# A planner of instruction order: transposing transfers that hold the queue, DRAM stores ordered with their loads, a limit on adding transfers, and new ranks

## The chip, the cores and the metric

The kernel runs on one core of a Trainium2 chip. The metric is the device time of one execution in microseconds (us); the time of a kernel is the median of its runs.

The engines are TensorE (PE in the profile; its weight loads are PEld), VectorE (DVE), ScalarE (ACT), GpSimd (POOL) and SyncE (SP). Each executes its own instructions in the order in which they were written. SP issues nearly all transfers here and POOL the adding ones, so each of them has a queue too.

## The reference

The output is a sum of three terms over x, a matrix of 2048 tokens by 1024 channels:

```python
xn = _layernorm(x, axis=-1)
return x + _A_ref(xn, A_k, A_v, A_shift_k, A_ssm_k, A_ssm_D) + _B_ref(xn, B_w1, B_w2)
```

`_B_ref` is a feed-forward network, silu(xn · w1) · w2 with 3584 inner columns. `_A_ref` has a short causal convolution of k with four taps per channel, a product with v, a long causal convolution over the 2048 tokens per channel (by a Fourier transform of twice the length), and a product with xn:

```python
kv = k_shift * v
...
y_f = kv_f * kf_f[None, :, :, :]
...
y = y + kv * ssm_D[None, None, :]
return q * y
```

All values are 32-bit floats.

## The kernel before

**The work.** The two products of the feed-forward network are done on PE in 16-bit halves: each operand is split into a high and a low part, and each product is three matmuls (high·high, high·low, low·high; lines 1073 to 1075 for the first, 1228 to 1230 for the second). A scheme of seven products instead of eight for blocks of 2 by 2 stands around them, so that sums and differences of rows and of weights are made on DVE, split on ACT (high part) and DVE (low part), partly stored in DRAM (`xspS`, `xspA`, `ws_T`, `ws_B`, `hs`, `w2sP`) and loaded again. The first product's weights come as tiles `raw` (loads from `in_w`); ACT takes their sum of squares (`junk<-raw`), PE sums it over partitions (`ps<-ss,oneb`, line 506), and the split parts are called `wo`. The rows of x are normalised on DVE (`xt`, line 639) and turned on PE (line 658). `ht` and `hf` are tiles of the inner layer and of results.

The long convolution goes over eight groups of 128 channels. For one group `kin` (the padded k) and `kf` (the long filter) are loaded, ACT and DVE apply the taps to get `acc`, v is multiplied in, `hl` holds split parts, some of them turned by a transposing transfer (`hl<-cm`, line 376), PE does a first stage of the transform (lines 1800 to 1802, into `ps`, copied by ACT to `spec` and `tmp`), DVE multiplies the spectra, ACT and DVE split the result (`zh`, `zl`), PE does the inverse (lines 2016 to 2018), and DVE multiplies by the normalised rows `xg` to get `yt`, which POOL adds into `out` in DRAM. A result of the network (`hf`) is added likewise. A stage of the convolution is cut into short pieces that stand between the matmuls of the network; such a stretch, in which spectra are copied, is called a burst below.

**The order.** The program is not written in its final order. Pieces of work are generators ("streams") that yield operations, each an `Op` with its engine, a guess of its time (`busy`), of how much later its result can be read (`late`), what it reads and writes, and its bytes. `Order.run` keeps a clock for every engine, reckons for each stream when its next operation could start, takes the one with the smallest start minus the stream's rank (`bias`), and emits it. So the guesses and the ranks decide the order of every engine's list, and nothing else: what waits for what is decided by semaphores, from the tiles that an instruction reads and writes. The network's matmuls keep their sequence, and other work on PE is put in between.

Helpers make the operations: `L` a load or store on SP (line 355), `X` a transposing transfer on SP (line 376), `G` an adding transfer on POOL (line 380), `V` an operation on DVE (lines 384 and 387), `A` and `a_act` one on ACT (line 397), `T` one on PE. `convolution` starts the streams of the convolution, at the earliest at a time `floor`. In the changed kernel these lines have other numbers: 386, 407, 413, 422, 425 and 435.

Of the kernel before, what the change touches and what calls it, by code (L numbers as in the profile page):

```python
# [20 lines left out]
P = 128  # L21
# [72 lines left out]
class Op:  # L94


    def __init__(self, eng, busy, late, emit, reads, writes, margin, nbytes=0):
        self.eng, self.busy, self.late, self.emit, self.margin = eng, busy, late, emit, margin
        self.reads, self.writes, self.nbytes = reads, writes, nbytes
        self.table = None  # L100
        self.extra, self.rate = 0.0, 0.0


class Stream:
# [5 lines left out]
class Order:  # L110
# [7 lines left out]
    def __init__(self):  # L118
        self.free, self.count = defaultdict(float), defaultdict(int)
        self.wrote, self.read = {}, {}  # L120
        self.slots, self.patterns = {}, {}
        self.streams = []
        self.pipe = self.now = 0.0
        self.table = None

    def cells(self, a):

        if a.space == bass.MemoryType.DRAM:
            return ()
        dims = [tuple(d) for d in a.ap]  # L130
        item = mybir.dt.size(a.dtype)
        key = (a.offset % dims[0][0] if dims[0][0] else 0, tuple(dims[1:]), item)
        if key not in self.patterns:
            offs = np.array([key[0]])
            for step, n in dims[1:]:
                offs = (offs[:, None] + step * np.arange(n)[None, :]).reshape(-1)
# [21 lines left out]

    def prepare(self, s):
        op, t = s.head, -s.head.margin  # L160
        r = [c for a in op.reads for c in self.cells(a)]
# [12 lines left out]

    def run(self):
        while self.streams:
            for s in list(self.streams):
# [141 lines left out]
def h3_ffn_kernel(ctx, tc, x, kp, vs, fs, shift, dskip, w1, w2, cfwd, cinv, out):  # L319
# [26 lines left out]
    def A(f, o, ins, us=None, m=0.15):  # L346
        return Op("ACT", us or 0.1 + size(o) / 1200, 0.2, f, ins, [o], m)

    def T(f, o, ins, us, m=0.2):

        return Op("PE", us, 0.3, f, ins, [o], m)

    def L(o, i, m=0.3):
        n = size(o) * o.shape[0] * mybir.dt.size(o.dtype)
        return later(Op("SP", 0.4, 0.1, lambda: nc.sync.dma_start(o, i), [i], [o], m, n), 0.0, along(o, i, 43.5, 53, 96))

    def later(p, extra, ns):
        p.extra, p.rate = extra, ns * 1e-3 / 16 / 1024
        return p
# [13 lines left out]
    def X(o, i, m=0.3):  # L373

        n = size(o) * o.shape[0] * mybir.dt.size(o.dtype)
        return later(Op("SP", 0.6, 4.0, lambda: nc.sync.dma_start(o, i, transpose=True), [i], [o], m, n), 0.2, 97)

    def G(o, i, m=0.3):
        n = size(i) * i.shape[0] * mybir.dt.size(i.dtype)
        return later(Op("POOL", 1.1, 2.5, lambda: nc.gpsimd.dma_start(o, i, accum_op=ADD), [i], [o], m, n), 0.3,  # L380
                     along(o, i, 83, 119))

    def v_tt(o, a, b, op, **k):
        return V(lambda: nc.vector.tensor_tensor(o, a, b, op=op), o, [a, b], **k)  # L384
# [565 lines left out]
    def quad(i, sp):  # L950
# [26 lines left out]
        add(factors(("S3", "S1"), flat[1], (ltok,)), 0.1)  # L977
        yield v_tt(x, v, x, SUB)
        ltok.set()
        yield v_tt(y, y, x, SUB)  # L980
# [456 lines left out]
    def copies():  # L1437
        n = NT // 2
        for a in range(NT):
            yield flag["unit", a // 2] if a < n else flag["result", a - n + 4]  # L1440
            q = slice(a % n * 2 * P, (a % n + 1) * 2 * P), slice(a // n * W, (a // n + 1) * W)
            o = out[q]
            yield later(Op("SP", 0.4, 0.1, lambda: nc.sync.dma_start(o, x[q]), [], [], 0.3, P * D * 4), 0.0, 43.5)
            flag["copied", a // n].set()

    def squares_w2():
# [92 lines left out]
        flag["all raw"].set()  # L1539

    CLAIM = 5
    SB = 0.04

    def load_w2f():

# [80 lines left out]
                       ap=[list(a.ap[0])] + [list(d) for d in dims] + [[1, n * P]])  # L1626

    TO = (1, 3, 0, 2)
    BETWEEN = (0, 1, 2, 3, 4, 5, None, None, None, 6, 7, None, None, 8, None, None)

    def convolution(floor):
        ra = late.enter_context(tc.tile_pool(name="ra", bufs=1))
# [17 lines left out]
        def rest(floor):  # L1650
# [8 lines left out]
            ctxs["wraw"] = Halves(order, rb, "wraw", 1)  # L1659
            ctxs["squares"] = [(ctxs["wraw"], more["yt"])[:1 + (i < NP // 2)] for i in range(NP)]  # L1660
            add(copies(), 0.3)
            for gen, bias in ((result_parts(), 0.05), (stage1_inv(), 0.03), (norm_rows(), 0.0), (norms_w2(), 0.14)):
                add(gen, bias, max(order.free["DVE"], order.free["ACT"]))

        def loads():
# [376 lines left out]
                if t == tiles2[-1][1]:  # L2042
                    flag["conv out"].set()

        for gen, bias in ((loads(), 0.05), (load_v(), 0.04), (gate(), 0.02), (signal_parts(), 0.07), (parts_of(), 0.14), (stage1(), 0.2),
                          (transforms(), 0.02), (squares_w2(), 0.0), (rest(floor), 0.0)):
# [113 lines left out]
```

## Time and profile before

| what | value |
|---|---|
| median of three runs | 1239.15 us (1236.41 to 1239.62) |
| profiled execution | 1237.35 us, of which the span 1235.6 us |
| busy: PE, DVE, ACT, POOL | 1217.4, 1135.2, 747.2, 143.9 us |
| granted clock of PE | 1.00 |
| transfers | 312.09 MB, 253 GB/s over the span |

The span is the time from the first to the last instruction that the profile shows. Busy time is the sum of an engine's instructions, so an engine can be the bound and still be idle for short waits; those are in the chain of waits and in the brackets of the timeline's rows. Rows of SP marked SPq show when its queue issued a transfer and how long the issue held it, and not when the data landed.

### The profile page before, as it was taken

The page shows a single profiled execution, that of the slowest core. Times are in us where ns is not written, and L with a number is a line of the kernel's source. Part 1 is how long each engine was busy: PE and PEld are TensorE (multiplying, and loading weights), DVE is VectorE, ACT ScalarE, POOL GpSimd, SP SyncE. Part 2 cuts the span into 40 slices and gives each one's busy share as a digit, 9 for nine tenths or more (in the row PEclk, how much of TensorE's full clock was granted, in tenths as well). Part 3 has the DMA queues.
Part 4 walks back from the last instruction along what each step waited for, and adds up shares of the span by engine and source line. Part 5 has one row for each costly group of instructions (what it writes and reads, how often), then busy time and mean ns, then how long its engine had stood idle before and what let it go on. Part 6 is the DMA issues. An engine that isn't in the chain of part 4 may idle for free.

```text
span 1235.6 us, 17325 instructions
## 1 busy us (share of the span) xinstructions
PE 1217.4 (99%) x6092; PEld 591.3 (48%) x6093; DVE 1135.2 (92%) x1414; ACT 747.2 (60%) x1299; POOL 143.9 (12%) x164
## 2 busy tenths in 40 slices
PE   8999998999999999999999999999999999999998
PEld 7644444444444454445444444454444445445445
DVE  7998995988799989999999999999998997997993
ACT  7867886887767796767764464353345337336232
POOL 2000000000000020001110130021013014112213
PEclk9999999999999999999999999999999999999999
DMA  9368889889999999987999899989969978776667
GB/s 339 108 208 308 295 299 306 279 267 317 337 371 307 286 252 305 271 238 223 306 361 282 262 296 286 236 222 285 279 142 234 331 164 198 179 159 131 152 144 140
DMA packets 264295, 312.09 MB, mean 253 GB/s; under 512 B 49424, under 2 KB 175632, under 8 KB 261136
## 3 DMA queue, kind: packets, MB, share of 16 engines
q1 hardware_dynamic: 237616, 286.33, 73.0%
q0 software_dynamic: 26592, 24.65, 14.4%
q8 instruction: 47, 0.77, 0.2%
q14 instruction: 40, 0.33, 0.1%
HBM read 198.20 MB, written 112.72 MB: 252 GB/s over the span
## 4 chain that ended last, share of the span: by engine, by line
PE 59%; DVE 19%; DMA 10%; issue 6%; ACT 5%; POOL 1%; SPq 0%; ACTq 0%; DVEq 0%; POOLq 0%
PE ff L1075 9%; PE ff L1073 9%; PE ff L1074 9%; PE ff L1228 9%; PE ff L1229 9%; PE ff L1230 9%; DVE spec L384 5%; DVE wo L387 2%; DMA raw<-in_w 2%; DMA hsfA<-ht 2%; DVE ht L387 2%; DVE tmp L384 1%; PE ps L1800 1%; PE ps L1802 1%; PE ps L1801 1%
## 5 line engine op out<-in xcount | busy, mean ns | idle before, releaser
L1075 PE MATMUL ff<-x,wo 128*128 128x512 f16 (+2 forms) x840 | 306.8, 367 | 2.3 <-DVE wo L387 2.3
L1074 PE MATMUL ff<-x,wo 128*128 128x512 f16 (+2 forms) x840 | 306.8, 367 | 1.4 <-DVE x L387 1.4
L1073 PE MATMUL ff<-x,wo 128*128 128x512 f16 (+2 forms) x840 | 306.7, 367 | 0.7 <-ACT wo L397 0.4
L1228 PE MATMUL ff<-x,wo 128*128 128x512 f16 x778 | 292.3, 376 | 0.4 <-ACT hf L397 0.4
L1229 PE MATMUL ff<-x,wo 128*128 128x512 f16 x778 | 292.3, 376 | 0.0
L1230 PE MATMUL ff<-x,wo 128*128 128x512 f16 x778 | 292.2, 376 | 0.0
L384 DVE TENSOR_TENSOR spec<-spec 128x512 f32<-128x512 f32 (+1 forms) x280 | 246.1, 914 | 0.7
L1230 PEld LDWEIGHTS <-wo 128*128 128x128 f16 x860 | 84.1, 98 | 99.4
L1228 PEld LDWEIGHTS <-wo 128*128 128x128 f16 x860 | 84.1, 98 | 98.9 <-issue 0.2
L1229 PEld LDWEIGHTS <-wo 128*128 128x128 f16 x860 | 84.1, 98 | 98.1 <-issue 0.6
L1075 PEld LDWEIGHTS <-wo 128*128 128x128 f16 x840 | 82.1, 98 | 95.0 <-DVE wo L387 3.1
L1073 PEld LDWEIGHTS <-wo 128*128 128x128 f16 x840 | 82.1, 98 | 92.1 <-issue 3.4
L1074 PEld LDWEIGHTS <-wo 128*128 128x128 f16 x840 | 82.1, 98 | 87.1 <-issue 1.2
L380 POOL DMA_DIRECT2D out<-yt x62 | 68.9, 1323 | 346.9 <-DVE yt L387 322.9
L380 POOL DMA_DIRECT2D out<-hf x61 | 56.7, 929 | 421.5 <-ACT hf L397 324.2
L397 ACT ACTIVATE hf<-ff,invc 128x512 f32<-128x512 f32 x62 | 42.2, 681 | 94.9 <-PE ff L1230 76.3
L384 DVE TENSOR_TENSOR tmp<-spec 128x2048 f32<-128x2048 f32 (+1 forms) x48 | 92.2, 1931 | 0.5
L384 DVE TENSOR_TENSOR spec<-tmp 128x512 f32<-128x512 f32 (+1 forms) x96 | 80.1, 864 | 0.5
L387 DVE SCALAR_TENSOR_TENSOR ht<-hf,wsc,ht 128x1024 f16<-128x1024 f32 (+1 forms) x56 | 65.3, 1166 | 10.7 <-ACT ht L397 8.0
L387 DVE SCALAR_TENSOR_TENSOR wo<-raw,wsc,wo 128x512 f16<-128x512 f32 (+1 forms) x56 | 56.2, 1013 | 14.2 <-ACT wo L397 13.9
L397 ACT ACTIVATE ht<-hf,wsc 128x1024 f16<-128x1024 f32 (+1 forms) x56 | 59.0, 1054 | 8.8 <-DVE hf L384 4.3
L397 ACT ACTIVATE spec<-spec 128x1024 bf16<-128x1024 f32 x32 | 33.7, 1054 | 50.1 <-DVE spec L384 41.0
(193 smaller groups left out, 1869.4 us busy)
## 6 DMA issues: line engine op xcount, KB each, us to landing
wo<-hs SPq DMA_DIRECT2D x128, 256.0 KB, 5.3
wraw<-in_w SPq DMA_DIRECT2D x33, 512.0 KB, 6.1
hs<-ht SPq DMA_DIRECT2D x64, 256.0 KB, 4.8
out<-hf POOLq DMA_DIRECT2D x61, 256.0 KB, 5.2
raw<-in_w SPq DMA_DIRECT2D x28, 512.0 KB, 6.1
kin<-in_kp SPq DMA_DIRECT2D x16, 704.0 KB, 6.4
w2sP<-wo SPq DMA_DIRECT2D x42, 256.0 KB, 4.4
kf<-in_fs SPq DMA_DIRECT2D x8, 1024.0 KB, 6.4
```

Of the source, the lines that this page charges most:

```text
L380: return later(Op("POOL", 1.1, 2.5, lambda: nc.gpsimd.dma_start(o, i, accum_op=ADD), [i], [o], m, n), 0.3, along(o, i, 83, 119))
L384: return V(lambda: nc.vector.tensor_tensor(o, a, b, op=op), o, [a, b], **k)
L387: p = V(lambda: nc.vector.scalar_tensor_tensor(o, a, s, b, op0=op0, op1=op1), o, [a, b] + ([] if isinstance(s, float) else [s]), **k)
L397: nc.scalar.activation(o, i, func, scale=scale, **kw)
L1073: nc.tensor.matmul(o, w[:, 0, k], xf[:, :, k, 0], start=first and k == 0, stop=False, **kw)
L1074: nc.tensor.matmul(o, w[:, 0, k], xf[:, :, k, 1], start=False, stop=False, **kw)
L1075: nc.tensor.matmul(o, w[:, 1, k], xf[:, :, k, 0], start=False, stop=last and k == KH - 1, **kw)
L1228: nc.tensor.matmul(o, hx[:, 0, :], wc[:, 0, q], start=begin, stop=False, **kw)
L1229: nc.tensor.matmul(o, hx[:, 0, :], wc[:, 1, q], start=False, stop=False, **kw)
L1230: nc.tensor.matmul(o, hx[:, 1, :], wc[:, 0, q], start=False, stop=end, **kw)
L1800: nc.tensor.matmul(o, cf[:, 0], hi[i], start=i == 0, stop=False, **kw)
L1801: nc.tensor.matmul(o, cf[:, 0], lo[i], start=False, stop=False, **kw)
```

## The change

The change touches the planner alone: its guesses, its ranks, and what it takes for a dependence. The instructions are the same ones, save three fewer of the spare matmuls with which PE is kept busy at the start; their order differs. There are four parts.

- DRAM: the planner's list of what was read and written (`cells`) knew on-chip memory only. Now stores to scratch tensors and to `out` count too, with `dram`, so that a load of what was stored is planned behind its store. An adding transfer is planned behind the copy of x into `out` (`after`).
- Adding transfers: at most 768 rows of them are planned in flight (`room`, `ring`).
- Guesses: a transposing transfer has 1.3 instead of 0.6 us on SP, and holds SP in the plan until the transfers ahead of it have drained (`held`); loads 0.5 instead of 0.4; adding transfers 0.6 instead of 1.1 on POOL.
- Ranks: many `bias` values, and the table `BETWEEN`, which sets between which matmuls the pieces of the first transform stage stand. `convolution` now starts only when the last reads of the pools that it replaces are planned to be over.

```diff
     def cells(self, a):
 
+        dims = [tuple(d) for d in a.ap]
         if a.space == bass.MemoryType.DRAM:
-            return ()
-        dims = [tuple(d) for d in a.ap]
+            return self.dram(a, dims)
...
+    def dram(self, a, dims):
+
+        name = a.tensor.name
+        if name.startswith("in_"):
+            return ()
+        if name.startswith("out_"):
+            row, col = divmod(a.offset, D)
+            if dims[0][0] == D:
+                return [("copied", row // (2 * P), col // W)]
+            at = [(row % T2 + T2 // 2 * i, row // HALF) for i in range(2 if len(dims) > 2 else 1)]
+            return [(name, t, b, col // P + c) for t, b in at for c in range(max(1, dims[-1][1] // P))]
+        offs = {a.offset + P * i for i in range((dims[-1][1] + P - 1) // P)}
+        for step, k in dims[:-1]:
+            if k != P:
+                offs = {o + step * i for o in offs for i in range(k)}
+        return [(name, o) for o in offs]
...
+    def room(self, t, rows):
+
+        held = [q for q in self.ring if q[0] > t]
+        while held and sum(n for _, n in held) + rows > 6 * P:
+            t = max(t, held.pop(0)[0] + 0.3)
+        return t
...
                     t = max(self.free[e] + late, s.at)
+                    if s.head.rows:
+                        t = self.room(t, s.head.rows)
...
+                if op.held:
+                    op.busy = max(op.busy, self.pipe - 0.35 - t)
+                if op.rows:
+                    self.ring = [q for q in self.ring if q[0] > t] + [(end, op.rows)]
...
-    def T(f, o, ins, us, m=0.2):
+    def T(f, o, ins, us, m=0.1):
...
-        return later(Op("SP", 0.4, 0.1, lambda: nc.sync.dma_start(o, i), [i], [o], m, n), 0.0, along(o, i, 43.5, 53, 96))
+        return later(Op("SP", 0.5, 0.1, lambda: nc.sync.dma_start(o, i), [i], [o], m, n), 0.0, along(o, i, 43.5, 53, 96))
...
-        return later(Op("SP", 0.6, 4.0, lambda: nc.sync.dma_start(o, i, transpose=True), [i], [o], m, n), 0.2, 97)
+        p = later(Op("SP", 1.3, 3.3, lambda: nc.sync.dma_start(o, i, transpose=True), [i], [o], m, n), 0.2, 97)
+        p.held = True
+        return p
...
-            yield (0.25, 0.2, 0.1, 0.14)[min(n, 3)]
+            yield (0.25, 0.2, 0.1, 0.04)[min(n, 3)]
...
-    BETWEEN = (0, 1, 2, 3, 4, 5, None, None, None, 6, 7, None, None, 8, None, None)
+    BETWEEN = (0, 1, 2, None, 3, 4, 5, None, 6, None, 7, None, None, 8, None, None)
...
-            for gen, bias in ((result_parts(), 0.05), (stage1_inv(), 0.03), (norm_rows(), 0.0), (norms_w2(), 0.14)):
+            for gen, bias in ((result_parts(), 0.05), (stage1_inv(), 0.03), (norm_rows(), 0.05), (norms_w2(), 0.3)):
...
-        convolution(max(order.free["DVE"], order.free["ACT"]))
+        ids = {id(r) for r in (xts_r, sums_r, s1_r, xst_r)}
+        left = [t for k, t in order.read.items() if isinstance(k[0], tuple) and k[0][0] in ids]
+        convolution(max([order.free["DVE"], order.free["ACT"]] + left))
...
-        add(more_rows(), 0.0)
+        add(more_rows(), 0.3)
...
-    add(transposes(), 0.05)
+    add(transposes(), 0.0)
...
-    add(factors_w1(), 0.1)
-    add(spill_w1(), 0.04)
+    add(factors_w1(), 0.05)
+    add(spill_w1(), 0.02)
```

What this does to the lists is shown at three places. In their rows a name with a number is a tile, `A<-B` is written from read, and x2 stands for two alike in succession.

The first is SP's list at the start of the convolution, near 190 us of the profile before. Before:

```order
L355 DMA ws_T_125<-wo_205 128x1024
L355 DMA raw_2157<-in_w 128x4x256
L355 DMA xspA_155<-xst_2079 128x1024
L355 DMA xspS_157<-xst_2080 128x1024
L355 DMA kin<-in_kp 128x1408
L355 DMA hs_88<-ht_214 128x4x256 x2
L355 DMA kf<-in_fs 128x2048
L355 DMA raw_2210<-in_w 128x4x256
L355 DMA ws_T_126<-wo_209 128x1024
L355 DMA ws_B_127<-wo_205 128x1024
L355 DMA hs_89<-ht_215 128x4x256 x2
```

After:

```order
L386 DMA raw_2152<-in_w 128x4x256
L386 DMA xspS_153<-xst_2050 128x1024
L386 DMA xspA_155<-xst_2081 128x1024
L386 DMA xspS_157<-xst_2082 128x1024
L386 DMA hs_88<-ht_214 128x4x256 x2
L386 DMA raw_2205<-in_w 128x4x256
L386 DMA ws_T_126<-wo_206 128x1024
L386 DMA ws_B_127<-wo_207 128x1024
L386 DMA kin<-in_kp 128x1408
L386 DMA hs_89<-ht_215 128x4x256 x2
L386 DMA kf<-in_fs 128x2048
```

The second `raw` of these rows stood behind kin, a pair of hs stores and kf, and now stands ahead of kin and kf, right behind the pair; one spill store (`xspS_153`) moved behind the first `raw`.

The second is ACT's list in the fifth burst of the convolution (group 4, near 930 us). Before:

```order
L397 ACTIVATE tmp<-ps_8187 128x2x256
L397 ACTIVATE tmp<-ps_8192 128x2x256
L397 ACTIVATE xg_8152<-xg_8152,nmr,rstd 128x128
L397 ACTIVATE spec<-ps_8187 128x2x256
L397 ACTIVATE xg_8152<-xg_8152,nmr,rstd 128x128
L397 ACTIVATE spec<-ps_8192 128x2x256
L397 ACTIVATE tmp<-ff_8224 128x2x256
L397 ACTIVATE xg_8152<-xg_8152,nmr,rstd 128x128 x2
L397 ACTIVATE tmp<-ps_8231 128x2x256
L397 ACTIVATE spec<-ff_8224 128x2x256
```

After:

```order
L435 ACTIVATE tmp<-ps_8204 128x2x256
L435 ACTIVATE tmp<-ps_8209 128x2x256
L435 ACTIVATE spec<-ps_8204 128x2x256
L435 ACTIVATE spec<-ps_8209 128x2x256
L435 ACTIVATE tmp<-ff_8239 128x2x256
L435 ACTIVATE tmp<-ps_8245 128x2x256
L435 ACTIVATE spec<-ff_8239 128x2x256
L435 ACTIVATE spec<-ps_8245 128x2x256
L435 ACTIVATE xg_8257<-xg_8257,nmr,rstd 128x128 x2
```

The rows of xg, which wait for a load, stood among the copies of the transform's results, and now stand behind all of them. In the burst of group 3 it is the other way round: there all four xg rows stood ahead of the last two copies only, and now two of them stand ahead of eight copies, and two ahead of the last four; the load of these two stands on SP behind a transposing transfer and the load of kf.

The third is DVE's list at the start, near 10 us. Before:

```order
L602 BN_STATS st<-xt_249 128x6
L387 SCALAR_TENSOR_TENSOR x_232<-ft_309,x_232 128x4x128
L602 BN_STATS st<-xt_249 128x6
L545 TENSOR_SCALAR pow_322<-ft_321 128x1
L547 RECIPROCAL pow_322<-pow_322 128x1
L605 BN_AGGR ln_226<-st 128x2
L387 SCALAR_TENSOR_TENSOR x_233<-ft_329,x_233 128x4x128
L639 TENSOR_SCALAR xt_249<-xt_249,ln_226 128x1024
L387 SCALAR_TENSOR_TENSOR wo_205<-x_238,wsc,wo_205 128x512
L602 BN_STATS st<-xt_263 128x6 x2
L387 SCALAR_TENSOR_TENSOR wo_205<-x_238,wsc,wo_205 128x512
```

After:

```order
L640 BN_STATS st<-xt_251 128x6 x2
L583 TENSOR_SCALAR pow_315<-ft_314 128x1
L585 RECIPROCAL pow_315<-pow_315 128x1
L643 BN_AGGR ln_226<-st 128x2
L425 SCALAR_TENSOR_TENSOR x_232<-ft_298,x_232 128x4x128
L425 SCALAR_TENSOR_TENSOR x_233<-ft_322,x_233 128x4x128
L677 TENSOR_SCALAR xt_251<-xt_251,ln_226 128x1024
L425 SCALAR_TENSOR_TENSOR wo_205<-x_238,wsc,wo_205 128x512 x2
```

The second half of the row's statistics (BN_STATS) moved ahead of the split of x, and those of the next row are no longer between the two wo rows.

At the tail, SP's list ended in two xg loads, two loads `hf<-out` and two xg loads, and now has the second pair of xg between the two `hf<-out`. On DVE and ACT near 70 us, the split of ht stood ahead of a split wo, and now stands behind it. In the list of PE the pieces of the convolution and the turns of rows stand at other places between the network's matmuls, by up to some microseconds of matmul work.

More of the change, by code (lines that the diff above doesn't have):

```diff
@@ L100, in __init__ @@
         self.table = None
-        self.extra, self.rate = 0.0, 0.0
+        self.extra, self.rate, self.rows, self.held, self.after = 0.0, 0.0, 0, False, []
 class Stream:
@@ L123, in __init__ @@
         self.pipe = self.now = 0.0
+        self.ring = []
         self.table = None
     def cells(self, a):
+        dims = [tuple(d) for d in a.ap]
         if a.space == bass.MemoryType.DRAM:
-            return ()
-        dims = [tuple(d) for d in a.ap]
+            return self.dram(a, dims)
         item = mybir.dt.size(a.dtype)
@@ L160, in prepare @@
         op, t = s.head, -s.head.margin
-        r = [c for a in op.reads for c in self.cells(a)]
+        r = [c for a in op.reads for c in self.cells(a)] + op.after
         w = [c for a in op.writes for c in self.cells(a)]
@@ L375, in X @@
         n = size(o) * o.shape[0] * mybir.dt.size(o.dtype)
-        return later(Op("SP", 0.6, 4.0, lambda: nc.sync.dma_start(o, i, transpose=True), [i], [o], m, n), 0.2, 97)
+        p = later(Op("SP", 1.3, 3.3, lambda: nc.sync.dma_start(o, i, transpose=True), [i], [o], m, n), 0.2, 97)
+        p.held = True
+        return p
     def G(o, i, m=0.3):
         n = size(i) * i.shape[0] * mybir.dt.size(i.dtype)
-        return later(Op("POOL", 1.1, 2.5, lambda: nc.gpsimd.dma_start(o, i, accum_op=ADD), [i], [o], m, n), 0.3,
-                     along(o, i, 83, 119))
+        p = later(Op("POOL", 0.6, 3.0, lambda: nc.gpsimd.dma_start(o, i, accum_op=ADD), [i], [o], m, n), 0.3,
+                  along(o, i, 83, 119))
+        p.rows = n // (mybir.dt.size(o.dtype) * o.shape[-1])
+        if o.space == bass.MemoryType.DRAM:
+            row, col = divmod(o.offset, D)
+            p.after = [("copied", row // HALF * (NT // 4) + a, col // W) for a in range(NT // 4)]
+        return p
     def v_tt(o, a, b, op, **k):
@@ L976, in quad @@
         yield v_tt(z, x, z, SUB)
-        add(factors(("S3", "S1"), flat[1], (ltok,)), 0.1)
+        add(factors(("S3", "S1"), flat[1], (ltok,)), 0.07)
         yield v_tt(x, v, x, SUB)
@@ L1442, in copies @@
             o = out[q]
-            yield later(Op("SP", 0.4, 0.1, lambda: nc.sync.dma_start(o, x[q]), [], [], 0.3, P * D * 4), 0.0, 43.5)
+            yield later(Op("SP", 0.6, 0.1, lambda: nc.sync.dma_start(o, x[q]), [], [o], 0.3, P * D * 4), 0.0, 43.5)
             flag["copied", a // n].set()
@@ L1541, in h3_ffn_kernel @@
     CLAIM = 5
-    SB = 0.04
+    SB = 0.07
     def load_w2f():
@@ L2043, in gated @@
                     flag["conv out"].set()
-        for gen, bias in ((loads(), 0.05), (load_v(), 0.04), (gate(), 0.02), (signal_parts(), 0.07), (parts_of(), 0.14), (stage1(), 0.2),
+        for gen, bias in ((loads(), 0.05), (load_v(), 0.04), (gate(), 0.02), (signal_parts(), 0.07), (parts_of(), 0.1), (stage1(), 0.2),
                           (transforms(), 0.02), (squares_w2(), 0.0), (rest(floor), 0.0)):
```

## Prediction

> **What bounds the kernel now.** I read the page first: its busy times, then the waits of TensorE (PE), then the stretches, and then the rows at each wait.
>
> ```profile
> span 1235.6 us, 17325 instructions
> ...
> PE 1217.4 (99%) x6092; PEld 591.3 (48%) x6093; DVE 1135.2 (92%) x1414; ACT 747.2 (60%) x1299; POOL 143.9 (12%) x164
> ```
>
> PE is the bound, with 18.2 us of the span in which it isn't busy. An order can win only there, at a clock that is full in every stretch that I show. The waits of PE (line, what it waited for, total us, times, longest) name where most of these 18 us lie:
>
> ```profile
> PE ps L506 <- ACT junk L397: 3.1, 1, 3.1
> PE ff L1075 <- DVE wo L387: 2.3, 3, 1.3
> PE ps L1800 <- DVE tmp L384: 1.6, 1, 1.6
> PE ff L1074 <- DVE x L387: 1.4, 2, 1.0
> PE ft L658 <- DVE xt L639: 1.0, 2, 0.8
> PE ps L2017 <- DVE zl L387: 0.8, 1, 0.8
> PE ps L1800 <- ACT spec L397: 0.8, 1, 0.8
> PE ft L658 <- DVE s L387: 0.7, 2, 0.4
> PE ft L658 <- ACT xt L397: 0.7, 1, 0.7
> PE ff L1228 <- ACT hf L397: 0.4, 1, 0.4
> ```
>
> These ten are 12.8 us, and none is a transfer: each is VectorE (DVE) or ScalarE (ACT) being late, sometimes because a transfer held them. The second limit is DVE, by stretches (us, then busy time and count of PE, PEld, DVE, ACT, POOL, the granted clock, the DMA share, GB/s):
>
> ```profile
> 210.00:330.00 120.00, 120.00 (x562) 54.40 (x560) 103.45 (x139) 98.45 (x164) 0.76 (x1) 1.00 0.95 297
> 330.00:480.00 150.00, 149.75 (x719) 70.09 (x718) 143.28 (x161) 114.98 (x197) 9.70 (x9) 1.00 1.01 310
> 480.00:780.00 300.00, 299.23 (x1440) 140.18 (x1438) 294.29 (x342) 181.77 (x309) 33.21 (x34) 1.00 0.95 278
> ```
>
> From 210 to 480 us PE is full and DVE has 23 us free; from 480 to 780 us DVE has 5.7 us left in 300.
>
> **The change part by part.** It adds and removes no work but three spare warm-up matmuls on a PE that waits there anyhow (cost zero, and covered by the wait for the first data). Every other instruction stays; the planner's guesses and ranks only put it elsewhere. So the sum goes by waits that open or close.
>
> *The load behind kin (208 us).* First the rows of SyncE (SP, start and us), whose queue issues the loads, then ACT's (in brackets its idle time before and what ended it), PE's, and the page's row on this kind of load (KB each, median us to landing):
>
> ```profile
> 189.19 0.43 SPq L355 DMA_DIRECT2D xspS<-xst  x1
> 194.75 0.33 SPq L355 DMA_DIRECT2D kin<-in_kp  x1
> 195.17 0.93 SPq L355 DMA_DIRECT2D hs<-ht  x2
> 196.16 0.66 SPq L355 DMA_DIRECT2D kf<-in_fs  x1
> 196.91 1.05 SPq L355 DMA_DIRECT2D raw<-in_w  x1
> ```
>
> ```profile
> 206.94 1.06 ACT L397 ACTIVATE junk<-raw 128x1024 bf16<-128x1024 f32 x1 [7.09 <-DMA raw<-in_w]
> ```
>
> ```profile
> 204.66 0.38 PE L1075 MATMUL ff<-x,wo 128*128 128x512 f16 x1
> 208.14 0.16 PE L506 MATMUL ps<-ss,oneb 128*128 128x2 bf16 x1 [3.10 <-ACT junk L397]
> ```
>
> ```profile
> raw<-in_w SPq DMA_DIRECT2D x28, 512.0 KB, 6.1
> ```
>
> SP stands from 189.62 to 194.75 before kin, because kin takes memory of the last spill store; raw goes out four places behind it, lands after 10.0 us (196.91 to 206.94) where the median of its 28 kind is 6.1, and ACT stands idle 7.09. In the new order raw goes ahead of kin, right behind the first hs pair. Its issue then is near 191.5, an estimate: 189.19 + 0.43, plus the hs pair of 0.93, plus the wait for its producer. It lands at 197.6 (median) to 201.5 (the 10.0 us of this row); junk ends 1.06 later, by 202.6 at the latest, and PE comes there at 204.88 (204.66 and one step of the 0.216 at which these matmuls start). The wait is gone: 3.1 by the row. Ends: 0 (if another producer is as late) and 3.1. I take **−3.1**. kin and kf then go out last. The first to read either is ACT's square of kf:
>
> ```profile
> 212.01 1.06 ACT L397 ACTIVATE hl<-kf 128x1024 bf16<-128x1024 f32 x1 [0.89 <-issue]
> ```
>
> It stands 15.9 us behind kf's issue, and kf moves by three rows of under 1 us each, so I cost that at nothing.
>
> *The start.* DVE:
>
> ```profile
> 10.34 0.69 DVE L387 SCALAR_TENSOR_TENSOR x<-ft,x 128x512 f16<-128x512 f32 x1 [0.56 <-ACT xt L397]
> 14.76 1.28 DVE L602 BATCH_NORM_STATS2 st<-xt 128x6 f32<-128x512 f32 x2
> 15.95 0.73 DVE L387 SCALAR_TENSOR_TENSOR wo<-x,wsc,wo 128x512 f16<-128x512 f32 x1
> ```
>
> The second half of a row's statistics now fills the 0.56, and the 1.28 of the next row's stand behind the wo split that PE waits for (L1075 and L1074: 3.7 in five waits, two of the wo ones and one x before 21 us). DVE gains up to 1.84 at 15.95, but ACT's part of the split and the loads come no earlier. Ends 0 and −1.8; the middle, **−0.9**.
>
> *Row ht ahead of wo (70 us).*
>
> ```profile
> 68.86 1.28 DVE L387 SCALAR_TENSOR_TENSOR ht<-hf,wsc,ht 128x1024 f16<-128x1024 f32 x1
> 70.04 1.29 DVE L387 SCALAR_TENSOR_TENSOR wo<-raw,wsc,wo 128x1024 f16<-128x1024 f32 x1
> ```
>
> PE waits 1.3 for this wo (longest of L1075). It now stands ahead of ht on DVE and ACT, worth 1.18 (70.04 − 68.86) if its input is there. Ends 0 and −1.3; **−0.8**, nearer the row. What is late next is ht, whose readers are transfers.
>
> *Transposes (L658).* They wait 2.4 us in five places; the new order puts most of them 2 to 5 us of matmul time later, while new places arise. Ends +0.7 (the longest again) and −2.4; I take **−0.5**.
>
> *Bursts of the convolution* (stage 1, products and inverse of one channel group follow on one another). Group 4, ACT and then PE:
>
> ```profile
> 932.12 0.49 ACT L397 ACTIVATE xg<-xg,nmr,rstd 128x128 f32<-128x128 f32 x1 [3.13 <-DMA xg<-in_x]
> 933.87 0.38 PE L1800 MATMUL ps<-hl,cfw 128*128 128x512 f16 x1 [1.61 <-DVE tmp L384]
> ```
>
> ACT waits in order for a gate row xg while copies of PE's results (spec, tmp) stand behind it, and PE waits for those. In the new order all copies of that burst stand ahead of the xg rows: **−1.6** (ends 0 and −1.6). For the 0.8 at zl, PE comes 2.6 to 3.2 us of matmul time later to the same DVE work: **−0.7**. For the 0.8 at spec the place on PE is the same and DVE has slightly less ahead of it: **−0.4**, ends +0.8 and −0.8.
>
> *The tail.*
>
> ```profile
> 1210.40 7.31 SPq L355 DMA_DIRECT2D hf<-out  x2
> 1217.82 1.20 SPq L355 DMA_DIRECT2D xg<-in_x  x2
> 1222.68 0.88 ACT L397 ACTIVATE xg<-xg,nmr,rstd 128x128 f32<-128x128 f32 x2 [0.23 <-DMA xg<-in_x]
> 1223.46 0.67 ACT L397 ACTIVATE hf<-ff,invc 128x512 f32<-128x512 f32 x1
> ```
>
> The second hf load waits for an addition into out to land; the second xg pair stands behind it, and ACT's hf copy, for which PE waits 0.4, behind that. The pair now goes out between the two hf loads: **−0.4** (ends 0 and −0.4).
>
> *New waits.* No row shows them. The nearest row for an order of this kind is this one's own list: of its 12.8 us, 8.4 go above, and 4.4 stay. I let a fifth of what goes come back elsewhere, **+1.7**; ends 0 and all of it, +8.4.
>
> The limit on rows of adding transfers and the order of DRAM stores act on the list only; POOL's 143.9 us busy of 1235.6 can hide a later addition. Raising a transposing transfer's time on SP moves it and its neighbours by a place or so, costed at nothing at the x loads behind, and at its worst in the rivals.
>
> Sum: −3.1 −0.9 −0.8 −0.5 −1.6 −0.7 −0.4 −0.4 +1.7 = −6.7. The profiled run took 1237.35 for a span of 1235.6; with the change 1230.65. The median of the runs is 1239.15, 1.8 above the profiled one, so the forecast is **1232.4**.
>
> **The rivals.** A (gives back): PE comes 5.3 us earlier (the terms before 330 us) to a stretch in which DVE has 5.7 us free in 300. If DVE is what sets the pace there, the lead ends at a burst, as a longer wait for spec, zl or tmp: −6.7 + 5.3 = −1.4, so 1237.8. For it speaks the 294.29 of 300; against it the 23 us that DVE has free from 210 to 480, in which the earlier start can be taken along.
>
> B (slower): a transposing transfer holds SP, and a load that ACT needs inside a burst stands behind it.
>
> ```profile
> 310.37 9.67 SPq L376 DMA_TRANSPOSE hl<-cm  x1
> 704.51 1.52 SPq L376 DMA_TRANSPOSE hl<-cm  x1
> 716.51 0.88 ACT L397 ACTIVATE xg<-xg,nmr,rstd 128x128 f32<-128x128 f32 x2 [0.34 <-DMA xg<-in_x]
> ```
>
> These are two holds on SP and, of group 3 before, ACT's xg row. In group 3 the new order puts the second xg load behind a transposing one and the 1 MB kf, and its row on ACT ahead of the burst's last four copies; before, the xg rows stood ahead of the last two alone. With the usual 1.5 nothing is lost; with 9.67 SP and ACT are 8.15 later, and of an ACT wait of 3.13 PE saw 1.61 at 933 us, so 1.5 is hidden and 6.6 reaches PE. Slower by more than 3.7 needs 10.4 on top of the sum, so two such holds (13.2): −6.7 + 13.2 = +6.5, 1245.7; one gives 1239. Against it: at 704 us, in this very group, the hold was 1.52. [...]
>
> C (another producer is as late at 208 us): the first term falls, −3.6, 1235.5. Against it the ACT row, idle 7.09 for raw alone.
>
> D (nothing happens): the terms are moved by less than they are worth, 1239. The five terms above that rest on a named place in the order are against it.
>
> **How the numbers follow.** About 0.3%, 3.7 us, is what a measurement of this kernel can tell from no change. Forecast, −10 to −4 us: 0.60, and 0.06 more beyond it; A 0.17; C 0.05; D 0.04; B 0.08. Faster: forecast with what lies beyond (0.66) and half of C, 0.68; slower: B, 0.08, and some of the +8.4 end of new waits, 0.10 in all; the rest, 0.22, is within. The range from 1226.9 (every term at its gaining end and no new wait, −12.2) to 1239.5 (D, or one hold of B) leaves 2 in 10 out.
>
> **What would show it.** In the profile after: ACT's 7.09 and PE's 3.1 at 208 us are gone, with raw ahead of kin on SP; no xg row of ACT idles inside group 4's burst; the first matmul waits before 21 us are shorter by near 1; hf at the tail doesn't wait for xg; DVE's busy time stays at 1135. It is wrong if PE's waits for spec, tmp, zl or wo between 480 and 1000 us grow by more than 3 us (A or B), or if SP's transposing rows of 5 us and more stand ahead of an xg that ACT waits for.

## The result and the profile after

The changed kernel took 1232.66 us (median of six runs, 1229.4 to 1233.87), the kernel before beside it 1239.18 (1236.41 to 1241.98): a ratio of 0.9945, 95% interval 0.9927 to 0.9963. That is 6.5 us less; 1232.4 had been forecast. The profiled execution of the changed kernel took 1233.5 for a span of 1231.7, so the two profiles are only 3.9 us apart. The page of the changed kernel (span; busy time, share and count by engine), and then PE's waits:

```profile
span 1231.7 us, 17303 instructions
...
PE 1215.8 (99%) x6089; PEld 590.7 (48%) x6090; DVE 1136.5 (92%) x1414; ACT 750.8 (61%) x1299; POOL 143.7 (12%) x164
```

```profile
PE ff L1111 <- ACT hf L435: 2.6, 4, 1.2
PE ff L1112 <- DVE x L425: 2.2, 3, 0.9
PE ft L696 <- DVE xt L677: 2.0, 1, 2.0
PE ff L1113 <- DVE wo L425: 1.5, 3, 0.8
PE ps L1838 <- DVE yt L425: 1.3, 1, 1.3
```

The waits for junk (3.1 us), tmp (1.6), zl and spec (0.8 each) are gone from the list. The waits for hf (2.6), yt (1.3) and xt (2.0, at 9.45 us, ahead of the network's first matmul) are new or longer. At 208 us SP's rows show raw ahead of kin and kf, and ACT has no idle time for it (its row stands below them):

```profile
190.72 1.59 SPq L386 DMA_DIRECT2D hs<-ht  x2
192.40 0.74 SPq L386 DMA_DIRECT2D raw<-in_w  x1
193.19 0.84 SPq L386 DMA_DIRECT2D ws_T<-wo  x1
194.12 0.46 SPq L386 DMA_DIRECT2D ws_B<-wo  x1
195.75 0.33 SPq L386 DMA_DIRECT2D kin<-in_kp  x1
```

```profile
198.62 1.06 ACT L435 ACTIVATE junk<-raw 128x1024 bf16<-128x1024 f32 x1
```

One pair of profiles doesn't show where the time went, because single executions of one order differ by up to 2.7 us in a stretch. The experiments below leave most of either order as it was, and so each gave one more execution of it. The table has the time between the same two matmuls of the network, taken from the timelines (in the first row, from the start of the span to such a matmul); a stretch is named by its place in the profile before. A star marks a stretch that the edit of that run changes, left out of the last column.

| stretch, us | before | before_less_dve, xg_last (order of before) | after | raw_last, after_less_dve (order of after) | means, after − before |
|---|---|---|---|---|---|
| 0 to 29 | 28.34 | 28.38, 28.23 | 28.14 | 26.82, 26.92 | −1.0 |
| 29 to 54 | 25.72 | 25.71, 25.71 | 26.87 | 26.86, 26.86 | +1.15 |
| 54 to 87 | 32.04 | 32.04, 32.04 | 30.98 | 30.98, 30.98 | −1.06 |
| 87 to 195 | 108.64 | 107.08, 109.59 | 109.01 | 107.91, 107.32 | −0.4 |
| 195 to 238 | 43.24 | 45.03, 42.63 | 39.98 | 48.75*, 39.98 | −3.65 |
| 238 to 485 | 246.19 | 248.01*, 248.88 | 246.72 | 247.23, 246.59* | −0.6 |
| 485 to 510 | 25.10 | 25.06*, 25.11 | 26.85 | 27.07, 25.06* | +1.86 |
| 510 to 691 | 181.60 | 181.60, 181.61 | 181.69 | 181.56, 181.56 | 0.0 |
| 691 to 741 | 50.20 | 50.61, 50.79 | 51.04 | 50.34, 53.01* | +0.2 |
| 741 to 914 | 172.20 | 172.61, 171.74 | 171.74 | 171.74, 171.74 | −0.4 |
| 914 to 949 | 35.06 | 34.44, 32.62* | 32.22 | 32.22, 32.22 | −2.5 |
| 949 to the end | 280.43 | 281.11, 282.58 | 279.91 | 280.89, 279.91 | −1.1 |

The last column adds up to about −7.5 us, where the medians are 6.5 apart; with two or three executions of each order, whose stretches differ by up to 2.7 us, it can't be closer. Most of it comes from two places, near 208 and near 933 us, and 1 us each from the start and from 70 us; 1.15 us is lost at 30 us and 1.9 at 490 us.

### The profile page after: what moved, and what is told of

The parts are those of the page before. It is cut to its first block, busy times and chain, and to the rows that moved or that the text cites. A ratio compares the mean times of both kernels' runs of the same rounds, so it can differ in the third digit from the quotient of the medians.

```text
span 1231.7 us, 17303 instructions
## 1 busy us (share of the span) xinstructions
PE 1215.8 (99%) x6089; PEld 590.7 (48%) x6090; DVE 1136.5 (92%) x1414; ACT 750.8 (61%) x1299; POOL 143.7 (12%) x164
## 4 chain that ended last, share of the span: by engine, by line
PE 71%; DVE 11%; issue 8%; DMA 6%; ACT 3%; POOL 1%; SPq 0%; DVEq 0%; POOLq 0%; ACTq 0%
PE ff L1266 12%; PE ff L1268 12%; PE ff L1267 12%; PE ff L1111 9%; PE ff L1113 9%; PE ff L1112 9%; PE ps L1838 2%; PE ps L1840 2%; PE ps L1839 2%; DMA raw<-in_w 2%; DVE spec L422 2%; DVE x L425 1%; DVE ht L425 1%; DVE wo L425 1%; DMA out<-yt 1%
## 5 line engine op out<-in xcount | busy, mean ns | idle before, releaser
L413 POOL DMA_DIRECT2D out<-hf x61 | 54.2, 888 | 420.4 <-ACT hf L435 323.5
L425 DVE SCALAR_TENSOR_TENSOR acc<-kin,taps,acc 128x1024 f32<-128x1024 f32 x48 | 61.3, 1277 | 1.4 <-ACT acc L435 1.3
```

The lines of the kernel that those rows point to most:

```text
L413: p = later(Op("POOL", 0.6, 3.0, lambda: nc.gpsimd.dma_start(o, i, accum_op=ADD), [i], [o], m, n), 0.3, along(o, i, 83, 119))
L425: p = V(lambda: nc.vector.scalar_tensor_tensor(o, a, s, b, op0=op0, op1=op1), o, [a, b] + ([] if isinstance(s, float) else [s]), **k)
```

## The experiments

Those that move one instruction use a small addition to the planner: the plan is made as ever, and a marked operation is emitted only when so many later operations of an engine have gone out. All other rows keep their places. Line numbers in these kernels are larger by the lines added.

```diff
-            op.emit()
+            self.send(op)      # emits op, or keeps it until p.hold = (engine, n) is counted down
```

### The load behind kin

**raw_first**, one move in the kernel before:

```diff
-                    yield L(kin, kp[g, b])
+                    yield hold(L(kin, kp[g, b]), "SP", 3) if (g, b) == (0, 0) else L(kin, kp[g, b])
...
-                        yield L(kf, fs[g])
+                        yield hold(L(kf, fs[g]), "SP", 1) if g == 0 else L(kf, fs[g])
```

> The kernel before with one move: on SP, kin and kf of the first group stand behind the raw load that PE waits for at 208 us; every other row of every engine is in its place. Theory 'terms add' (a wait taken away before 330 us stays away): PE's wait of 3.1 us at ps (sum of squares) is gone, ACT's 7.09 too, and the kernel is 3 us faster (1236). Rival 'given back': PE comes 3 us earlier to 460 to 505 us, DVE does not, and PE waits there for ACT's hf or DVE; the kernel is 0 to 1 us faster. Rival 'another producer' (C of the prediction): the wait stays, on another name, no change.

Measured: 0.9995 of before (0.9982 to 1.0009), so no change. The wait at 208 is gone. Nine us later PE stands for 2.53 us. ACT's and PE's rows of raw_first:

```profile
211.61 1.06 ACT L415 ACTIVATE hl<-kf 128x1024 bf16<-128x1024 f32 x1 [5.00 <-issue]
```

```profile
216.97 0.38 PE L1091 MATMUL ff<-x,wo 128*128 128x512 f16 x1 [2.53 <-ACT hf L415]
```

ACT now reaches its square of kf early and stands there until 211.61. The profile names nothing that it waits for. What lies just ahead is POOL's addition of a row into kf, issued at 205.72, after kf had landed. Of this addition the second row below gives the time from issue to landing, 5.8 us, so it lands at 211.5, and the square starts at 211.61:

```profile
205.72 1.03 POOL L394 DMA_DIRECT2D kf<-in_dskip  x1 [104.91 <-DMA hs<-ht]
...
kf<-in_dskip POOLq DMA_DIRECT2D x1, 0.5 KB, 5.8
```

In the kernel before it is the same: the addition is issued at 206.15 and takes 5.8 us, and the square starts at 212.01.

All later rows of ACT, the copy hf among them, stand behind that square. Of the three expectations the second and third had the time right, but the lead was lost at 217 us and not at 460.

**raw_and_square** moves that square ten rows later on ACT as well:

```diff
+                    yield hold(p, "ACT", 10) if (g, a) == (0, 0) else p
```

> The kernel before with two moves: raw ahead of kin and kf on SP (as in raw_first), and on ACT the first square of kf ten rows later, where the changed kernel has it. In raw_first PE's wait at 208 us was gone and one of 2.69 us at 216.97 stood in its place, for hf, behind that square, which waited for POOL's addition into kf until 211.6. Theory 'the kf chain held ACT': the wait near 217 us goes to under 0.5, and 3 us of the lead hold at least to 330 us. Whether they hold to the end: 'terms add' 1237 against 1240 before, a ratio of 0.9975; 'given back at 460 to 505' a ratio of 0.9995 with 2 to 3 us of waits for hf there. If ACT is late for another reason, a wait of 2 us or more is left at 217.

Measured: 1.0001 (0.9986 to 1.0016). PE again waits, 2.51 us at 216.05, because the next raw load is now the late one, as ACT's row shows:

```profile
213.76 1.06 ACT L415 ACTIVATE junk<-raw 128x1024 bf16<-128x1024 f32 x1 [4.61 <-DMA raw<-in_w]
```

In this profile, the slowest of its twelve executions (1243.34 against a median of 1239.3), PE also ran at half its clock behind the wait (0.50 from 217.10 to 220.51, which is 1.7 us more; the last section has the rows).

**kin_late** holds kin and kf back until that pair of raw loads is out too (12 and 10 issues instead of 3 and 1).

> The kernel before with kin and kf of the first group held on SP until three raw loads have gone out (twelve and ten issues later), and the first square of kf ten rows later on ACT; nothing else moves. In raw_and_square the second pair of raw loads was the next to be late (213.76, behind 1.7 MB of kin and kf). Theory 'the loads share one supply, and the last of the row is late': both waits (208 and 216 us) are under 0.5, the lead near 230 us is 5 us (2.7 more than raw_and_square and 3.2 more than before). Rival: the square of kf, now waiting for its late load and POOL's addition, holds ACT and a wait of 2 to 4 us stands near 220. By the end, 2 to 3 us faster (0.998) if the lead is kept, 1.000 if it is given back between 330 and 505 us.

Measured: 0.9990 (0.9974 to 1.0006). The stretch from 195 to 238 us took 41.43 us, against 43.24 before, 44.33 in raw_and_square and 39.98 after. A wait of 1.29 us was left at 221.13. So the stretch is 1.8 us shorter than before, where I had expected 3.2: three moves together bring half of what the changed order has here. In this run POOL's addition also goes out only behind the two squares of kf (218.8 against 217.4 and 218.4), so that they don't wait for it. By the time alone the run can't be told from the kernel before.

**raw_last** undoes the move in the changed kernel: its raw load is held back for six issues, behind kin and kf.

```diff
+            yield hold(p, "SP", 6) if (n, a) == (10, 1) else p
```

> The changed kernel with the same move undone: its raw load stands behind kin and kf again, nothing else moves. 'Terms add': 3 us slower than the changed kernel, about 1236. 'Given back': PE's wait at 208 us is back with 3 us, the waits for hf between 460 and 505 us (2.9 us) are gone, and the time stays that of the changed kernel, 1232 to 1233.

Measured: 1.0012 of before (0.9997 to 1.0028), where the changed kernel is at 0.9945. The loss is over twice what either theory gave: 8.8 us in the stretch. The waits for hf between 460 and 505 us are not gone, as 'given back' has it, but as long as in the changed kernel (27.07 in that stretch). PE's row, and then its clock by stretches (us, busy time of the engines, the granted clock, the DMA share, GB/s):

```profile
205.14 0.16 PE L562 MATMUL ps<-ss,oneb 128*128 128x2 bf16 x1 [5.49 <-ACT junk L453]
```

```profile
205.00:211.00 6.00, 5.54 (x14) 1.97 (x14) 4.56 (x9) 3.10 (x10) 0.00 (x0) 0.50 0.49 138
211.00:214.00 3.00, 3.00 (x15) 1.37 (x14) 1.59 (x2) 2.26 (x3) 0.00 (x0) 0.99 0.77 221
```

The wait itself is 5.5 us, and after it PE runs for 6 us at half its clock, which is 3 us more. So in the changed order this one position is worth 8.8 us, and in the order of before it is worth nothing that the time shows: there the wait only goes on to the next late row.

**left_only** and **no_left**: the later start of the convolution alone in the kernel before, and the changed kernel without it. Both are planned anew.

```diff
-        convolution(max(order.free["DVE"], order.free["ACT"]))
+        convolution(max([order.free["DVE"], order.free["ACT"]] + left))
```

> The kernel before with one part of the change alone: the streams of the convolution start only when the last reads of the pools that they replace are planned to be over; ranks, guesses and DRAM order are those of before. It moves raw ahead of kin and starts the convolution's ACT rows later, and the whole order behind is planned anew. If this part carries the gain at 208 us, PE's wait there is gone and none stands at 217; by itself 3 to 5 us faster than before (ratio 0.996 to 0.9975) where nothing new opens, and 0.9990 to 1.000 where it is given back.

> The changed kernel without the later start of the convolution alone (its raw load stands behind kin and kf again, as in before), all else as changed, planned anew. If that part carries most of the gain: PE's wait at 208 us is back with 3 us or more, with some us at half clock if it is longer than 3.4, and the ratio to before is 0.998 to 1.000. If ranks and guesses carry it: 0.995 to 0.997 as the changed kernel.

Measured: 1.0077 (1.0056 to 1.0098) and 1.0072 (1.0045 to 1.0099): both are 9 us slower than before. Both expectations missed. In no_left raw does stand behind kin and kf, but PE's wait there is only 0.32 us (at 204.39). The 3.4 us of its expectation lie between two measured pauses, 3.26 in the kernel before (full clock behind it) and 3.43 in before_less_dve (half clock); a wait of 0.32 says nothing on it. In left_only the gain at 208 us is there (3.3 us by 213 us of before); half of it is gone by 230, nearly all by 400, and by 640 us the run is 12 us behind, in waits for hf, tmp and x. The later start is not a part that carries the gain by itself; as both runs have another order throughout, they don't show what it is worth inside the changed one.

### Where time is lost near 490 us

**after_less_dve** and **before_less_dve** leave out four of the six additions of taps of group 2 (5.1 us of DVE near 470 to 490 us), in the changed kernel and in the one before:

```diff
+                        if g == 2 and j > 0:
+                            p.emit = lambda: None
```

> The changed kernel without four of the six additions of taps of group 2 on DVE (between 467 and 490 us, 1.28 us each, 5.1 us of DVE; they are left out of the result). If DVE sets the pace from 460 to 505 us, PE's waits for hf there (2.9 us) shrink to under 0.7 and the kernel is 2 to 3 us faster than the changed one (about 1230). If ACT's own row of copies makes them, they stay within 0.5 us and so does the time.

> The kernel before without the same four additions of taps of group 2. PE has no wait of over 0.2 us between 460 and 700 us there, so if DVE is late only when PE leads, nothing changes (1239, within 1 us). If less DVE work helps in any case (later bursts come earlier), it is 1 to 2 us faster.

Measured: 0.9918 (0.9899 to 0.9937) and 0.9998 (0.9983 to 1.0013). In the changed kernel the waits for hf go, all but one of 0.85 us, and the stretch from 485 to 510 is back at 25.06. In the order of before nothing comes of it. So DVE sets the pace there in the changed order and not in the order of before. That it does so because PE leads, which is rival A's mechanism, is another matter: in raw_last PE comes to this place 6.9 us later than in the changed kernel and 4.4 us later than in the kernel before (the matmul at 485.03 of before, at 489.41), and its waits for hf are all there. So it is the order, and not the lead. By time the run is about 3 us below the changed kernel, with intervals that overlap; by the profile part of the lead is given back at the burst near 712 us, where PE now waits 2.6 us for yt instead of 1.3.

```profile
PE ps L1841 <- DVE yt L425: 2.6, 1, 2.6
PE ff L1112 <- DVE x L425: 2.2, 3, 0.9
PE ff L1113 <- DVE wo L425: 2.0, 4, 0.8
...
PE ff L1111 <- DVE hf L422: 0.8, 1, 0.8
```

The rows for x and wo are waits ahead of 71 us. The wait for yt has a cause of its own in the changed kernel, by DVE's rows at both places:

```profile
462.81 0.75 DVE L425 SCALAR_TENSOR_TENSOR yt<-ps,csc,xg 128x512 f32<-128x512 f32 x1 [2.85 <-DMA xg<-in_x]
...
714.77 0.75 DVE L425 SCALAR_TENSOR_TENSOR yt<-ps,csc,xg 128x512 f32<-128x512 f32 x1 [2.24 <-DMA out<-yt]
```

The second names the addition of the previous yt into out. There is one buffer for yt, in two halves, and DVE can't write it before POOL's transfer has read it. For the first the profile names an xg load, but its tile had been normalised by 457.4, and what ends just ahead of the row is again an addition: issued at 454.25, it landed at 462.63. (The second was issued at 705.89 and landed at 714.68.) The same row in raw_last, and in the kernel before:

```profile
469.67 0.75 DVE L439 SCALAR_TENSOR_TENSOR yt<-ps,csc,xg 128x512 f32<-128x512 f32 x1 [3.35 <-DMA xg<-in_x]
...
458.87 0.75 DVE L387 SCALAR_TENSOR_TENSOR yt<-ps,csc,xg 128x512 f32<-128x512 f32 x1 [0.39 <-DMA out<-yt]
```

In the six executions of the order of before this addition took 4.7 to 6.4 us from issue to landing, and DVE stood 0.29 to 2.05 us; in three of the changed order it took 8.4 to 8.9 us, and DVE stood 2.85 to 3.57. The 2.05 was in raw_first, where PE then waited for hf as well (0.91 us at 483.13 and 0.50 at 507.12), without a lead. Why the addition lands later in the changed order stays open; from 440 to 470 us all transfers together moved 296 GB/s there, and 255 in the kernel before.

**no_additions** leaves these additions out for the groups whose bursts stand there:

```diff
+                if g in (0, 2):
+                    p.emit = lambda: None
```

> The changed kernel without POOL's additions of yt into out for the first and third groups (near 440 to 464 and 704 to 720 us; these sums are left out of the result, 16 transfers of 128 KB); nothing else moves. Theory 'the one yt buffer sets DVE late': DVE's waits at yt (2.85 us at 462.81, 2.24 at 714.77) go, and with them PE's waits for hf between 460 and 505 (2.9 us) and most of the 1.46 at 715.57; 3 to 4 us faster than the changed kernel, ratio near 0.992. Rival 'DVE's own work': DVE's idle time goes elsewhere and PE's waits there stay over 2 us; ratio 0.994 to 0.995.

Measured: 0.9893 (0.9873 to 0.9912), some 6 us less than the changed kernel (0.9945), more than the 3 to 4 expected. Both DVE waits at yt are gone, and with them PE's:

```profile
457.86 0.74 DVE L425 SCALAR_TENSOR_TENSOR yt<-ps,csc,xg 128x512 f32<-128x512 f32 x1
```

```profile
PE ff L1112 <- DVE x L425: 2.2, 3, 0.9
PE ff L1113 <- DVE wo L425: 2.0, 4, 0.8
PE ft L696 <- DVE xt L677: 1.1, 1, 1.1
PE ff L2130 <- DVE oneb L482: 1.1, 1, 1.1
PE ps L2055 <- DVE zl L425: 0.6, 1, 0.6
```

No row for hf or for yt is left. DVE did the same work as in the changed kernel; it only did not stand at yt. So the time is lost where DVE, which has little free time, stands for the one yt buffer and its additions; less work on DVE or no wait at yt takes the loss away alike. What share of the 6 us comes from 2 MB fewer adding transfers on the DMA engines stays open.

### The burst of group 4

**xg_last** puts ACT's four xg rows behind the burst's copies in the kernel before. As one multiplication with xg comes ahead of them, it uses these rows before their normalising.

```diff
+                            yield hold(p, "ACT", (7, 6, 4, 4)[2 * b + i]) if (g, t) == (4, 2) else p
```

> The kernel before with one move: ACT's four xg rows of the burst of group 4 (near 932 us) stand behind all copies of that burst; nothing else moves. Prediction's term: PE's wait of 1.6 us at 933 us is gone and the kernel is 1.6 us faster (ratio 0.9987, hardly to be told from no change by time alone, so the wait in the profile decides). Rival: PE waits as long in the same burst for another copy or for yt, whose rows of xg are now later.

Measured: 1.0006 (0.9989 to 1.0023); the time alone can't tell 1.6 us. The stretch from 914 to 949 took 32.62, against 35.06 before and 32.22 after. ACT has no idle time for xg in it, and its idle rows there are behind PE:

```profile
932.73 1.25 ACT L415 ACTIVATE spec<-ps 128x512 f32<-128x512 f32 x2 [1.36 <-PE ps L1820]
935.33 0.60 ACT L415 ACTIVATE tmp<-ps 128x512 f32<-128x512 f32 x1 [0.71 <-PE ps L1820]
```

The same order, with xg in its old place, took 33.04 to 35.06 in five executions (33.04 in kin_late). Two waits make this spread: the one for tmp behind xg was 1.61, 1.51, 1.63, 1.60 and 0.66 us in these five, and is not there in xg_last; the one for zl, some 14 us ahead, was 0.83, 0.31, 0.47, 0.83 and none, and 0.16 in xg_last, whose edit doesn't touch it. So the move is worth 0.7 to 1.6 us, and the 1.6 of the forecast was near the upper end.

### The parts by themselves

**ranks_only** and **model_only** are the kernel before with the new ranks and BETWEEN alone, and with everything else of the change alone.

> The kernel before with the new ranks and the table BETWEEN alone; guesses, DRAM order and start of the convolution are those of before. The raw load stands behind kin and kf, so PE's wait at 208 us should be there with 3 us. If each part brings its share, the ratio is 0.997 to 0.999; if parts only fit together (as the two runs with and without the later start suggest, 1.0077 and 1.0072), it is over 1.003.

> The kernel before with the planner's new knowledge alone (DRAM order, limit on adding transfers, guesses, later start of the convolution), and the ranks of before. Its raw load goes ahead of kin and kf: no wait of over 0.7 us near 208 us. If the knowledge carries the gain, the ratio is 0.995 to 0.998; if ranks chosen for other guesses no longer fit, it is over 1.003.

Measured: 1.0123 (1.0099 to 1.0147) and 1.0032 (1.0016 to 1.0048): 15 and 4 us slower, where both together are 6.5 faster. Both have an order of their own throughout. The longest waits of ranks_only are of sizes that neither kernel has:

```profile
PE ff L1073 <- DVE hf L384: 5.9, 2, 4.7
PE ff L1073 <- ACT hf L397: 4.4, 5, 1.9
PE ff L1073 <- ACT x L397: 3.3, 1, 3.3
```

## Why the prediction was right, point by point

The total was right, 6.7 us forecast and 6.5 measured, and so was the direction of the change. Of its nine terms six were right at their places, one failed, one was too small, and one stays open. That the total came so close is in part luck: the new waits cost 3.0 us instead of 1.7, and some gains were larger than forecast.

- *The load behind kin*, −3.1: the stretch gained 3.65. The place was right. The reason was too short: the step that kin and kf cost nothing took the 15.9 us from kf's issue to its first reader at 212.01 for room. That reader stood for POOL's addition into kf (0.89 idle in its row), and so comes no earlier when raw does (raw_first). The changed order gains because the raw pair behind, the square of kf and kin all moved as well. Rival C, that another row is as late, is what happens if only the named row moves.
- *The start*, −0.9: the size and the place were right, though the two profiles hide it; what was to show it failed. In the profile after, the first weights of the network happened to come 0.9 us later:

```profile
7.06 0.69 DVE L835 BATCH_NORM_STATS2 wst<-x 128x6 f32<-128x512 f32 x1 [1.87 <-DMA x<-in_w]
...
7.98 0.69 DVE L873 BATCH_NORM_STATS2 wst<-x 128x6 f32<-128x512 f32 x1 [2.72 <-DMA x<-in_w]
```

  In raw_last and after_less_dve, of the same order, this row is at 6.68 and 6.69. Counted from it, the wo split that stood at 15.95 starts 8.89 us later before and 7.91 after (7.90 in raw_last), and the matmul at 28.34 comes 1.0 us sooner on average (the first row of the table). I had expected shorter waits of PE before 21 us; these stayed (1.45 us before; 1.41 after, and 0.41 more at 21.20), and the network started sooner instead. What I overlooked is right behind, as I had followed the new order to 21 us only: from 29 to 54 us 1.15 is lost in every execution of the changed order, so that nothing is left of the start's gain. PE now waits here:

```profile
31.40 0.27 PE L1112 MATMUL ff<-x,wo 128*128 128x256 f16 x1 [0.94 <-DVE x L425]
```

  DVE has four rows of statistics ahead of that split (27.77 to 30.22), and the turned rows that ACT and DVE split came late from PE (ACT stood 1.29 us for them until 29.54).
- *Row ht ahead of wo*, −0.8: −1.06. The wait at 71 us is 0.77 instead of 1.25, the one at 69.53 is gone.
- *Transposes*, −0.5: −0.4 between 87 and 195 us, where executions of one order differ by 2.5; neither shown nor refuted.
- *Group 4*, −1.6 and −0.7 for zl: −2.5 together. Right, with the spread above; by xg_last the first is 0.7 to 1.6. That zl gained by its later place on PE was not tested by itself.
- *spec at 703 us*, −0.4: the wait went, and one for yt came in the same burst; +0.2. The step that failed is that POOL's additions were costed at nothing, by its busy time, where it is their landing that the next yt waits for (8.8 us from issue in this burst).
- *Tail*, −0.4: hf waits for no xg there any more (its 3.03 idle at 1218.17 is for PE), and PE's wait of 0.35 is gone; the stretch of 280 us gained 1.1.
- *New waits*, +1.7: too small. +1.86 near 490 us and the +1.15 near 30 us are 3.0. The size was a guess, a fifth of what the other terms gain; the cause near 490 us, an adding transfer's buffer, had not been named.
- Rival A (0.17) named the stretch, and DVE's short free time plays a part in it, but its mechanism is not what the runs show: the loss of 1.9 us is there in raw_last too, where PE has no lead. What makes it is the yt buffer together with DVE's full list, in the changed order. Rival B didn't occur: the transposing transfer at the burst held SP 1.28 us (705.06), and the longest of all such holds went from 9.67 us to 3.52 (at 979.19). Rival D is refuted by the time itself, whose interval leaves out 1.

## What to carry to other kernels

A wait at the head of an in-order queue hides the waits behind it: taking away one late load, and then a second late row, gave nothing (ratios 0.9995 and 1.0001), and with a third moved too only half of the gain came (1.8 of 3.65 us in that stretch), so read the whole row of arrivals behind a wait before you book its length as a gain. Parts of an order are not terms of a sum; two halves of this change cost 4 and 15 us, and together they gain 6.5, so an order is measured whole. And price what releases a buffer by when it lands, not by how long the engine is busy that issued it: here a single output buffer stood behind an adding transfer that landed 8 to 9 us after its issue (8.8 for the one at 705.89, whose row on POOL took 1.1).

## What the runs showed of the hardware

In some executions the granted clock of PE fell to half behind a pause, and the pause cost more than its length. Pauses are counted here from start to start, less one step of 0.216. After 3.26 us at 208 us in the kernel before, PE went on at the full clock (1.00 from 208 to 211 us); after 3.43 us, in before_less_dve, it ran at half clock for some 3.4 us (an estimate from these rows: the second one's 0.55 leaves 0.24 of its 2.4 us at the full clock):

```profile
206.80:208.00 1.20, 1.20 (x4) 0.43 (x4) 0.60 (x1) 1.17 (x3) 0.00 (x0) 0.50 1.05 423
208.00:210.40 2.40, 2.40 (x8) 0.86 (x7) 1.40 (x2) 1.77 (x4) 0.00 (x0) 0.55 1.04 338
210.40:214.00 3.60, 3.60 (x18) 1.66 (x17) 1.51 (x5) 3.58 (x7) 0.00 (x0) 1.00 0.97 321
```

and after 5.66 us in raw_last for 6 us (0.50 from 205 to 211). This is a part of why executions of before differ by 2.4 us in that stretch (42.63 to 45.03, the latter in before_less_dve), and why the mean gain there is over 3.1.

Behind shorter pauses two runs differ. After one of 2.67 us (2.51 idle in its row at 216.05), raw_and_square has half clock from 217.10; after one of 2.69 (2.53 at 216.97), raw_first has the full clock:

```profile
217.10:220.51 3.41, 3.41 (x10) 1.24 (x9) 2.96 (x5) 3.17 (x5) 0.00 (x0) 0.50 0.72 234
...
218.93:222.34 3.41, 3.41 (x17) 1.56 (x16) 3.38 (x5) 3.41 (x9) 0.00 (x0) 1.00 0.95 234
```

In stretches of one length PE did 10 matmuls in the first and 17 in the second. So in these runs the length of a pause alone doesn't say whether the clock falls; what else decides it is not shown. In the forecast the 3.1 us of the wait could have been read as a risk of this kind, and were not.
